# Windowed attention on one core: two PSUM banks for the convolution, attention transposes in the main ring, patch loads among the other transfers, LN transposes one per slot

## The chip, the cores and the metric

The kernel runs on one core of one Trainium2 chip. The metric is the device time of one execution in microseconds (us): the median of two runs before the change is 7355.64 us (7354.11 to 7357.16). All times here are from those runs or from one profiled execution, which took 7363.1 us.

A core has five engines that run their own instruction queues in order: TensorE (PE in the profile; its weight loads are PEld), VectorE (DVE), ScalarE (ACT), GpSimd (POOL) and SyncE (SP), which in this kernel issues the DMA transfers. Engines wait for each other through semaphores. TensorE writes its results to PSUM; VectorE and ScalarE copy them to SBUF.

## The reference

The input is one image of 511 x 511 positions with 192 channels in bf16. A depthwise 3 x 3 convolution is added to it, each position is layer-normalised, and four-headed attention runs inside each of 73 x 73 windows of 7 x 7 positions:

```python
for i in range(kk):                      # kk = 3
    for j in range(kk):
        pe = pe + xp[:, i:i + H, j:j + W, :] * dw_pe[i, j][None, None, None, :]
x0 = x + pe
h = _layernorm(x0, axis=-1)
# ... h cut into windows of 49 positions: hw
qkv = (hw @ w_qkv).reshape(-1, ws * ws, 3, nh, dh)   # 4 heads of 48
attn = jnp.einsum('wnhd,wmhd->whnm', q, k) * scale
attn = _softmax(attn, axis=-1)
out = jnp.einsum('whnm,wmhd->wnhd', attn, v)
out = out.reshape(-1, ws * ws, C) @ w_o
# ... windows put back in place
return x0 + out
```

## The kernel before

Windows are taken in 42 blocks of up to 128, one window per partition. While one block is in attention, the convolution and the normalisation of the next are done beside it, and so is the output projection of the previous one. A block is cut into slots of eight windows, 16 in a full block and 667 in all.

PSUM holds three tiles of two banks in a ring (`PS`), one bank for the attention transposes and one for the convolution:

```python
self.PS = _Rot([psum.tile([128, 1024], F32, name=f"ps{i}") for i in range(3)])
self.PE_ = psum.tile([128, 512], F32, name="pse")
self.PC = psum.tile([128, 512], F32, name="psc")
```

The convolution of one channel is one matmul: the 81 values of a 9 x 9 patch per window against a table `T`. Ten channels fill the bank, and then VectorE copies it out:

```python
def conv_mm(cv):                                            # line 297 is the matmul
    c = cv.c
    mm(PCB[:, (c % 10) * S : (c % 10 + 1) * S], lhsT=XP[0:KP, :, c], rhs=T[0:KP, c, :], start=True, stop=True)
    cv.c += 1
    if cv.c % 10 == 0 or cv.c == C:
        ...
        nc.vector.tensor_copy(                              # line 302
            out=self.X[cv.b % 3][:, :, c0 : c0 + n], in_=PCB[:, 0 : n * S].rearrange("p (c s) -> p s c", s=S))
```

The patches `XP` come by 18 transfers per full block (line 265), all issued together once the convolution of the block in between has been read. The rows of x that are added to the convolution's result come through two buffers `xs` (line 279), and finished rows leave by stores (line 284). All three stand in SyncE's queue in program order.

The normalisation is a list of items, drawn from as the slots go: add a row of x (line 309, VectorE), statistics of two positions (line 313, VectorE), the inverse root by two Newton steps (lines 319 to 328), the multiply (line 336, GpSimd). Then `ln_tr` transposes eight positions on TensorE (line 350), and VectorE and ScalarE each copy one half out (line 359):

```python
def ln_rstd(i0, i1):
    e = nc.gpsimd
    e.tensor_scalar(out=t..., in0=v, scalar1=1.0 / C, scalar2=self.eps, op0=ALU.mult, op1=ALU.add)
    e = nc.vector
    e.tensor_scalar(out=rd.bitcast(I32), ..., op0=ALU.logical_shift_right)
    e.tensor_scalar(out=rd.bitcast(I32), ..., op0=ALU.mult, op1=ALU.add)
    e = nc.gpsimd
    for _ in range(2):
        e.tensor_tensor(out=u, in0=t, in1=rd, op=ALU.mult)
        e.tensor_tensor(out=u, in0=u, in1=rd, op=ALU.mult)
        e.tensor_scalar(out=u, in0=u, scalar1=-0.5, scalar2=1.5, op0=ALU.mult, op1=ALU.add)
        e.tensor_tensor(out=rd, in0=rd, in1=u, op=ALU.mult)
```

The stages of a slot, with what copies each out of PSUM: A (line 371, q then k; ScalarE, line 379), B (line 409, logits; ScalarE's exp into `pt`, line 417), V (line 387; ScalarE, line 395), D (line 430, attention times v; VectorE's reciprocal and multiply into `o`, lines 439 and 440), E (line 453, transposes of `o`; VectorE, line 454), and the projection of four positions (line 465; ScalarE, line 469, then GpSimd's add, line 473). D runs one slot after its B, E two slots after. Between the long matmuls of A, V and projection, `fill` puts convolution matmuls. The order in one slot `g`:

```python
stage_A(b, ck, 0, fill)
stats(0.2)
stage_A(b, ck, 1, fill)
stats(0.4)
stage_E(*groups[g - LE], nc.vector.tensor_copy)             # into the bank pse
for s0 in pj:
    proj(b - 1, s0, fill)
    ... store(b - 1, sdone)                                 # as soon as two rows are projected
stats(0.6)
stage_D()
stats(0.8)
stage_B()
stage_V(b, ck, fill, nc.scalar.copy)
while conv.c < conv_goal:                                   # conv_goal: part(0.0, 0.45, C)
    conv_mm(conv)
stats(1.0)                                                  # s_goal: part(0.47, 0.90, len(n.items))
if f > 0.71:
    n.transpose(7 if f == 1.0 else part(0.60, 1.0, 7))      # all that are due, in a row
if conv.c == C and xp_due:
    load_xp(b + 2)                                          # 18 transfers in a row
    xp_due = False
```

Of the kernel before, what the change touches and what calls it, by code (L numbers as in the profile page):

```python
# [61 lines left out]
class _Kernel:  # L62
    def __init__(self, ctx, tc, x, dw_pe, w_qkv, w_o, out, eps, logit_lim):
# [8 lines left out]
        self.PS = _Rot([psum.tile([128, 1024], F32, name=f"ps{i}") for i in range(3)])  # L72
        self.PE_ = psum.tile([128, 512], F32, name="pse")
        self.PC = psum.tile([128, 512], F32, name="psc")
        for t in self.PS.t + [self.PE_, self.PC]:
            nc.vector.memset(t[:], 0.0)
# [108 lines left out]
    def fast(self, ctx):  # L185
# [32 lines left out]
        mm = nc.tensor.matmul  # L218
        ebf = self.PE_[:].bitcast(BF)

# [9 lines left out]
        def clear(part, p0, n):  # L230

            nc.sync.dma_start(
                out=part[:, p0 : p0 + n, :], in_=bass.AP(tensor=zero.tensor, offset=zero.offset, ap=[list(zero.ap[0]), [0, n], [1, C]])
            )

        def load_xp(b):
            for a0, b0, da, db, n, p0 in blocks[b]:
                left = [0] if b0 == 0 else []
                right = [] if b0 + (n - 1) * db < NWC - 1 else list(range(n)) if da else [n - 1]
                if left and any(ln[1] for bb in blocks[:b] for ln in bb):  # L240
                    clear(XPr[0], p0, n if da else 1)
                if right and b:
                    clear(XPr[8], p0 + right[0], len(right))
                last = a0 + (n - 1) * da
                cuts = [0] + ([1] if da and a0 == 0 else []) + ([n - 1] if da and last == NWR - 1 else []) + [n]
                for i, j in zip(cuts, cuts[1:]):
                    if j <= i:
                        continue
                    top, bot = a0 + i * da == 0, a0 + (j - 1) * da == NWR - 1
                    if top and b:  # L250
                        clear(XP[0:9], p0 + i, j - i)
                    if bot and b:
                        clear(XP[KP - 9 : KP], p0 + i, j - i)
                    pr0, pr1 = (1 if top else 0), (8 if bot else 9)
                    for pc in range(9):
                        q, sh = (WS - 1, -1) if pc == 0 else (0, 1) if pc == 8 else (pc - 1, 0)
                        n0, n1 = i, j
                        if pc == 0 and left:
                            n0 = j if da else i + 1
                        if pc == 8 and right:  # L260
                            n1 = i if da else j - 1
                        if n1 <= n0:
                            continue
                        dims = [[W * C, pr1 - pr0], [WS * C * (W * da + db), n1 - n0], [1, C]]
                        nc.sync.dma_start(  # L265
                            out=XPr[pc, pr0:pr1, p0 + n0 : p0 + n1, :],
                            in_=dram(x, WS * (a0 + n0 * da) - 1 + pr0, WS * (b0 + n0 * db + sh) + q, dims),
                        )

# [25 lines left out]
        def conv_mm(cv):  # L295
            c = cv.c
            mm(PCB[:, (c % 10) * S : (c % 10 + 1) * S], lhsT=XP[0:KP, :, c], rhs=T[0:KP, c, :], start=True, stop=True)  # L297
            cv.c += 1
            if cv.c % 10 == 0 or cv.c == C:
                c0 = c - c % 10  # L300
                n = cv.c - c0
                nc.vector.tensor_copy(  # L302
                    out=self.X[cv.b % 3][:, :, c0 : c0 + n], in_=PCB[:, 0 : n * S].rearrange("p (c s) -> p s c", s=S)
                )
# [10 lines left out]
        def ln_rstd(i0, i1):  # L315
            e = nc.gpsimd
            v = bnst[:, i0:i1, :].rearrange("p a (e f) -> p a e f", f=3)[:, :, :, 2]
            rd, u, t = (z[:, 2 * i0 : 2 * i1] for z in (rstd, tmp1, tmp2))
            e.tensor_scalar(out=t.rearrange("p (a e) -> p a e", e=2), in0=v, scalar1=1.0 / C, scalar2=self.eps, op0=ALU.mult, op1=ALU.add)
            e = nc.vector  # L320
            e.tensor_scalar(out=rd.bitcast(I32), in0=t.bitcast(I32), scalar1=1, scalar2=None, op0=ALU.logical_shift_right)
            e.tensor_scalar(out=rd.bitcast(I32), in0=rd.bitcast(I32), scalar1=-1.0, scalar2=1597463007.0, op0=ALU.mult, op1=ALU.add)
            e = nc.gpsimd
            for _ in range(2):
                e.tensor_tensor(out=u, in0=t, in1=rd, op=ALU.mult)
                e.tensor_tensor(out=u, in0=u, in1=rd, op=ALU.mult)
                e.tensor_scalar(out=u, in0=u, scalar1=-0.5, scalar2=1.5, op0=ALU.mult, op1=ALU.add)
                e.tensor_tensor(out=rd, in0=rd, in1=u, op=ALU.mult)

# [116 lines left out]

        def stage_E(b, ck, eng):
            for kt in range(2):
                for Q in range(2):
# [5 lines left out]
                out=HO[b % 2][0:KT, :, ck * CH : (ck + 1) * CH, 0:S],  # L455
                in_=ebf[0:KT].rearrange("p (k w s) -> p k w s", k=2, s=64)[:, :, :, 0:S],
            )
# [36 lines left out]

        def load_chunk(b, k, tiles):
            tiles[k] = xs.next()
            load_x(b, k, tiles[k])

        groups = [(b, ck) for b in range(NB) for ck in range((count(b) + CH - 1) // CH)]
        NG = len(groups)  # L500
        LD, LE = 1, 2

        class Next:


            def __init__(n_, b):
                n_.b, n_.conv, n_.si, n_.loaded, n_.tr = b, Conv(b), 0, 0, 0
                n_.items, n_.tiles = stat_items(b)
                n_.ready = 0

# [6 lines left out]
            def stats(n_, goal):  # L517
                while n_.si < goal:
                    kind, it = n_.items[n_.si]
                    it()  # L520
                    n_.si += 1
                    if kind == 1:
                        n_.load()
                    n_.ready += kind == 2

            def transpose(n_, goal):
                while n_.tr < min(goal, n_.ready):
                    ln_tr(n_.b, 8 * n_.tr, n_.tr)
                    n_.tr += 1

        load_xp(0)
        n = Next(0)
# [4 lines left out]
        if NB > 1:  # L537
            load_xp(1)
        n.stats(len(n.items))
        n.transpose(7)  # L540

        for g in range(NG + LE + 1):
            b, ck = groups[g] if g < NG else (NB, g - NG)
            f0, f = 0.0, 1.0
            if g < NG:
                nslot = (count(b) + CH - 1) // CH
                f0, f = ck / nslot, (ck + 1) / nslot
            if ck == 0:
                n = Next(b + 1) if b + 1 < NB else None
                xp_due = b + 2 < NB  # L550
                pdone = sdone = 0

            def part(lo, hi, total):
                return min(total, max(0, int((f - lo) / (hi - lo) * total + 0.5)))

            pj = []
            if 1 <= b and ck >= LE:
                goal = 13 if b == NB else part(0.10, 0.70, 13)
                while pdone < goal:
# [3 lines left out]
            conv = n.conv if n else None  # L563
            conv_goal = part(0.0, 0.45, C)
            conv_start = conv.c if n else 0
# [8 lines left out]
            s_start = n.si if n else 0  # L574
            s_goal = part(0.47, 0.90, len(n.items)) if n else 0

            def stats(share):
                if n and conv.c == C:
                    n.stats(int(s_start + (s_goal - s_start) * share))

            if n and f >= 0.3 and n.loaded == 0:
                n.load()
                n.load()

            if g < NG:
                stage_A(b, ck, 0, fill)
                stats(0.2)
                stage_A(b, ck, 1, fill)
                stats(0.4)
            if 0 <= g - LE < NG:  # L590
                stage_E(*groups[g - LE], nc.vector.tensor_copy)
            for s0 in pj:
                proj(b - 1, s0, fill)
                while sdone < len(CHUNKS) and CHUNKS[sdone][1] * WS <= min(S, s0 + 4):
                    store(b - 1, sdone)
                    sdone += 1
                    stored[b - 1] = sdone
            stats(0.6)
            if 0 <= g - LD < NG:
                stage_D()  # L600
            stats(0.8)
            if g < NG:
                stage_B()
                stage_V(b, ck, fill, nc.scalar.copy)
                if n:
                    while conv.c < conv_goal:
                        conv_mm(conv)
                    stats(1.0)
                    if f > 0.71:
                        n.transpose(7 if f == 1.0 else part(0.60, 1.0, 7))  # L610
                    if conv.c == C and xp_due:
                        load_xp(b + 2)
                        xp_due = False

# [242 lines left out]
```

## Time and profile before

| Group | Instructions | Busy us | Mean ns |
|---|---|---|---|
| A, matmuls (line 371) | 5336 | 1825.0 | 478 |
| Convolution, matmuls (line 297) | 8064 | 1557.5 | 238 |
| V, matmuls (line 387) | 5336 | 923.2 | 303 |
| Projection, matmuls (line 465) | 4116 | 784.7 | 328 |
| E, matmuls (line 453) | 5336 | 636.2 | 291 |
| LN transposes, matmuls (line 350) | 4116 | 463.3 | 283 |
| Convolution copy, VectorE (line 302) | 840 | 541.8 | 645 |
| D copy, VectorE (line 440) | 667 | 638.7 | 958 |
| Statistics, VectorE (line 313) | 1050 | 544.8 | 549 |
| LN transpose copy, VectorE (line 359) | 294 | 337.8 | 1149 |
| q copy, ScalarE (line 379) | 667 | 541.7 | 812 |
| LN multiply, GpSimd (line 336) | 294 | 710.7 | 2435 |

Busy time is the sum over one kind of instruction, and the mean is that of one instruction; matmuls overlap each other, so their mean is longer than the step from one to the next. The granted clock of TensorE is a share of its full speed, 0.621 on average over the span. The transfers move 377.07 MB, 51 GB/s on average. A row of the waits names the engine and line that waited, what released it, the total in us, how often, and the longest.

### The profile page before, as it was taken

The numbers are of one execution on the slowest core, as the hardware profiler recorded it, in microseconds if no ns is written. First come the engines' busy times: TensorE is split into PE (matmuls) and PEld (weight loads), VectorE is DVE, ScalarE is ACT, GpSimd is POOL, SyncE is SP. The second block draws the span as 40 slices with busy tenths as digits, with TensorE's granted clock in tenths as the row PEclk, the third lists the DMA queues.
The fourth block names the chain that finished last, engine by engine and source line by source line (L and its number), as shares of the span: only waits on it lengthen the run. The fifth ranks groups of instructions, "written<-read, shape, count | busy, mean of one in ns | idle before, by whom it ended". The sixth has DMA issues, their size and how long they took to land.

```text
span 7363.1 us, 168522 instructions
## 1 busy us (share of the span) xinstructions
PE 5032.6 (68%) x75049; PEld 3971.4 (54%) x75049; DVE 2896.4 (39%) x4859; ACT 2853.6 (39%) x3521; POOL 1939.2 (26%) x2364
## 2 busy tenths in 40 slices
PE   1677777766777777777766777777777666666657
PEld 1555555555555555555555555555555555555445
DVE  4433433434443333334434444333444333333323
ACT  1333434433443433334433434344444333333325
POOL 3122222222222222222222222222222222222214
PEclk9866656665665666665656666555565655656557
DMA  2111212222211111122222211112122211111111
GB/s 61 36 49 49 53 49 53 58 65 60 53 51 49 49 49 49 50 53 53 62 63 60 53 49 49 49 49 53 49 54 62 60 45 46 46 47 47 43 32 39
DMA packets 529715, 377.07 MB, mean 51 GB/s; under 512 B 454181, under 2 KB 454373, under 8 KB 528979
## 3 DMA queue, kind: packets, MB, share of 16 engines
q1 hardware_dynamic: 528531, 365.92, 19.5%
q8 instruction: 589, 9.65, 0.5%
q14 instruction: 147, 1.20, 0.1%
q10 hardware_dynamic: 448, 0.30, 0.0%
HBM read 265.31 MB, written 100.27 MB: 50 GB/s over the span
## 4 chain that ended last, share of the span: by engine, by line
PE 52%; DVE 20%; SPq 16%; POOL 4%; issue 4%; DMA 3%; ACT 2%; DVEq 0%; POOLq 0%; ACTq 0%
PE ps L371 18%; SPq L265 14%; DVE X L302 6%; PE psc L297 6%; PE pse L453 6%; PE ps L387 6%; PE ps L350 6%; PE ps L465 6%; DVE HO L359 5%; DMA xs<-in_x_dram 3%; PE ps L430 3%; DVE HO L454 2%; DVE o L440 2%; POOL X L336 2%; PE ps L409 2%
## 5 line engine op out<-in xcount | busy, mean ns | idle before, releaser
L371 PE MATMUL ps<-HO,Wqk 96*128 96x392 bf16 x5336 | 1825.0, 478 | 992.8 <-DVE o L440 977.7
L297 PE MATMUL psc<-T,XP 81*128 81x49 bf16 x8064 | 1557.5, 238 | 494.4 <-DVE X L302 461.0
L473 POOL TENSOR_TENSOR X<-X,pO 128x768 bf16<-128x768 bf16 (+1 forms) x546 | 863.3, 1588 | 3306.3 <-ACT pO L469 3305.2
L371 PEld LDWEIGHTS <-Wqk 96*128 96x128 bf16 x5336 | 679.4, 132 | 1701.1 <-issue 1501.2
L297 PEld LDWEIGHTS <-XP 81*128 81x128 bf16 x8064 | 1337.0, 178 | 203.8 <-issue 114.1
L379 ACT CAST q<-ps 128x784 bf16<-128x784 f32 x667 | 541.7, 812 | 1403.3 <-PE ps L371 1326.0
L454 DVE COPY HO<-pse 96x784 bf16<-96x784 bf16 x667 | 382.0, 573 | 1559.7 <-PE pse L453 1559.7
L350 PE MATMUL ps<-ident,X 128*96 128x128 bf16 x4116 | 463.3, 283 | 723.1 <-DVE HO L359 423.0
L387 PE MATMUL ps<-Wv,HO 96*128 96x192 bf16 x5336 | 923.2, 303 | 35.3 <-ACT pO L469 35.3
L302 DVE CAST X<-psc 128x490 bf16<-128x490 f32 x840 | 541.8, 645 | 947.6 <-PE psc L297 942.2
L350 PEld LDWEIGHTS <-X 128*96 128x96 bf16 x4116 | 412.6, 175 | 738.2 <-issue 472.3
L465 PE MATMUL ps<-Wo,HO 96*128 96x192 bf16 x4116 | 784.7, 328 | 3.6 <-ACT pO L469 2.9
L395 ACT CAST v<-ps 128x768 bf16<-128x768 f32 x667 | 534.8, 802 | 525.5 <-PE ps L387 431.1
L387 PEld LDWEIGHTS <-HO 96*128 96x128 bf16 x5336 | 588.9, 121 | 252.7 <-issue 217.0
L336 POOL TENSOR_TENSOR X<-X,rstd 128x1536 bf16<-128x1536 bf16 (+1 forms) x294 | 710.7, 2435 | 13.1
L469 ACT CAST pO<-ps 128x768 bf16<-128x768 f32 x504 | 402.4, 799 | 782.8 <-PE ps L465 600.7
L465 PEld LDWEIGHTS <-HO 96*128 96x128 bf16 x4116 | 608.0, 176 | 180.9 <-issue 180.0
L417 ACT ACTIVATE pt<-ps 128x784 bf16<-128x784 f32 x667 | 550.3, 825 | 398.0 <-PE ps L409 396.0
L379 ACT CAST k<-ps 128x784 bf16<-128x784 f32 x667 | 542.2, 813 | 381.1 <-PE ps L371 345.6
L359 ACT COPY HO<-ps 96x1024 bf16<-96x1024 bf16 (+1 forms) x294 | 284.6, 968 | 976.1 <-PE ps L350 976.1
L309 DVE TENSOR_TENSOR X<-X,xs 128x1344 bf16<-128x1344 bf16 x294 | 293.5, 998 | 904.1 <-DMA xs<-in_x_dram 902.5
L440 DVE TENSOR_TENSOR o<-ps,rs 128x768 bf16<-128x768 f32 x667 | 638.7, 958 | 23.4
(59 smaller groups left out, 4163.1 us busy)
## 6 DMA issues: line engine op xcount, KB each, us to landing
XP<-in_x_dram SPq DMA_DIRECT2D x568, 216.0 KB
xs<-in_x_dram SPq DMA_DIRECT2D x574, 168.0 KB
out_dram<-X SPq DMA_DIRECT2D x246, 336.0 KB
XP<-in_x_dram SPq DMA_DIRECT2D x151, 212.6 KB
out_dram<-X SPq DMA_DIRECT2D x82, 168.0 KB
XP<-in_x_dram SPq DMA_DIRECT2D x16, 192.0 KB
XP<-in_x_dram SPq DMA_DIRECT2D x64, 30.4 KB
xs<-in_x_dram SPq DMA_DIRECT2D x63, 23.6 KB
```

What stands on the lines that cost most here:

```text
L265: nc.sync.dma_start(out=XPr[pc, pr0:pr1, p0 + n0 : p0 + n1, :], in_=dram(x, WS * (a0 + n0 * da) - 1 + pr0, WS * (b0 + n0 * db + sh) + q, d ...
L297: mm(PCB[:, (c % 10) * S : (c % 10 + 1) * S], lhsT=XP[0:KP, :, c], rhs=T[0:KP, c, :], start=True, stop=True)
L302: nc.vector.tensor_copy(out=self.X[cv.b % 3][:, :, c0 : c0 + n], in_=PCB[:, 0 : n * S].rearrange("p (c s) -> p s c", s=S))
L336: nc.gpsimd.tensor_tensor(out=hbuf(b)[:, s0:s1, :], in0=self.X[b % 3][:, s0:s1, :], in1=rstd[:, i : i + n].unsqueeze(2).to_broadcast([128, ...
L350: mm(pb[0:KT, kt * 1024 + i * 128 : kt * 1024 + (i + 1) * 128], lhsT=h[:, s0 + i, kt * KT : (kt + 1) * KT], rhs=ident[:], start=True, stop ...
L359: eng(out=HO[b % 2][0:KT, kt, :, s0 : s0 + N], in_=pb[0:KT, kt * 1024 : kt * 1024 + N * 128].rearrange("p (s w) -> p w s", w=128),)
L371: mm(ps[:, ab * 512 : ab * 512 + TOK], lhsT=self.Wqk[kt][0:KT, which * 2 + ab, :], rhs=HO[b % 2][0:KT, kt, ck * CH : (ck + 1) * CH, 0:S], ...
L379: nc.scalar.copy(out=dst[:, :, 0:TOK], in_=two_bank(ps, TOK))
L387: mm(ps[:, col : col + C], lhsT=HO[b % 2][0:KT, kt, w : w + 2, :].rearrange("p w s -> p (w s)"), rhs=self.Wv[kt][0:KT, :], start=(kt == 0) ...
L440: nc.vector.tensor_tensor(out=o_[:].rearrange("p b q (h d) -> p b (q h) d", d=DH), in0=ov[:, :, :, 0:DH], in1=r_[:].rearrange("p (b g) -> ...
L465: mm(ps[:, col : col + C], lhsT=HO[b % 2][0:KT, kt, :, s0 + i], rhs=self.Wo[kt][0:KT, :], start=(kt == 0), stop=(kt == 1))
L473: nc.gpsimd.tensor_tensor(out=xv, in0=xv, in1=o[:, 0:n, :], op=ALU.add)
```

## The change

The bank of the attention transposes is given to the convolution, which then alternates between two banks, and E takes a tile of the main ring. The patch loads become a generator whose transfers are issued a few at a time, from 0.44 to 0.92 of a block, and stores go out at the end of the slot that projected their rows. LN transposes go one per slot, before B, and only at least 0.9 slot after their multiply. The inverse root moves from GpSimd to VectorE, three fused instructions to a Newton step where there were four. The shares of the block for convolution, statistics and projection change a little. The purpose is that TensorE is not kept from its next matmuls by a copy, a burst or a queue.

The diff, cut to its core:

```diff
-        self.PE_ = psum.tile([128, 512], F32, name="pse")
-        self.PC = psum.tile([128, 512], F32, name="psc")
+        self.PC = _Rot([psum.tile([128, 512], F32, name=f"psc{i}") for i in range(2)])
...
         def load_xp(b):                                     # now a generator, clear() too
-                        nc.sync.dma_start(out=XPr[...], in_=dram(x, ...))
+                        yield lambda dst=dst, src=src: nc.sync.dma_start(out=dst, in_=src)
...
         def conv_mm(cv):
             c = cv.c
+            if c % 10 == 0:
+                cv.ps = PCB.next()
-            mm(PCB[:, (c % 10) * S : (c % 10 + 1) * S], lhsT=XP[0:KP, :, c], rhs=T[0:KP, c, :], ...)
+            mm(cv.ps[:, (c % 10) * S : (c % 10 + 1) * S], lhsT=XP[0:KP, :, c], rhs=T[0:KP, c, :], ...)
...
         def ln_rstd(i0, i1):
-            e = nc.gpsimd
+            e = nc.vector
             e.tensor_scalar(out=t..., in0=v, scalar1=1.0 / C, scalar2=self.eps, ...)
...
-            e = nc.gpsimd
             for _ in range(2):
-                e.tensor_tensor(out=u, in0=t, in1=rd, op=ALU.mult)
+                e.scalar_tensor_tensor(out=u, in0=rd, scalar=-0.5, in1=t, op0=ALU.mult, op1=ALU.mult)
                 e.tensor_tensor(out=u, in0=u, in1=rd, op=ALU.mult)
-                e.tensor_scalar(out=u, in0=u, scalar1=-0.5, scalar2=1.5, op0=ALU.mult, op1=ALU.add)
-                e.tensor_tensor(out=rd, in0=rd, in1=u, op=ALU.mult)
+                e.scalar_tensor_tensor(out=rd, in0=u, scalar=1.5, in1=rd, op0=ALU.add, op1=ALU.mult)
...
         def stage_E(b, ck, eng):
+            ebf = PS.next()[:].bitcast(BF)
...
-            def transpose(n_, goal):
-                while n_.tr < min(goal, n_.ready):
+            def transpose(n_, goal, age):
+                if n_.tr < min(goal, len(n_.ready)) and n_.ready[n_.tr] + age <= now[0]:
                     ln_tr(n_.b, 8 * n_.tr, n_.tr)
...
-            s_goal = part(0.47, 0.90, len(n.items)) if n else 0
+            s_goal = part(0.46, 0.82, len(n.items)) if n else 0
-            def stats(share):
+            def hook(share):
+                nonlocal xpn, sdone
+                at = f0 + (f - f0) * share
                 if n and conv.c == C:
                     n.stats(int(s_start + (s_goal - s_start) * share))
+                    if n.loaded < min(WS, n.added + 2):
+                        n.load()
+                while sq and sq[0][0] <= g + share:
+                    _, bb, k = sq.pop(0)
+                    store(bb, k)
+                    stored[bb] = k + 1
+                if conv is None or conv.c == C:
+                    goal = part(0.44, 0.92, len(xp), at)
+                    while xpn < goal:
+                        xp[xpn]()
+                        xpn += 1
...
+            late = f0 >= 0.44
             if g < NG:
                 stage_A(b, ck, 0, fill)
-                stats(0.2)
+                hook(0.15)
+            if 0 <= g - LE < NG:
+                stage_E(*groups[g - LE], nc.scalar.copy if late else nc.vector.tensor_copy)
+            if g < NG:
                 stage_A(b, ck, 1, fill)
-                stats(0.4)
-            if 0 <= g - LE < NG:
-                stage_E(*groups[g - LE], nc.vector.tensor_copy)
+                hook(0.35)
+            if 0 <= g - LD < NG:
+                stage_D()
             for s0 in pj:
                 proj(b - 1, s0, fill)
-                    store(b - 1, sdone)
+                    sq.append((g + 0.9, b - 1, sdone))
-            stats(0.6)
-            if 0 <= g - LD < NG:
-                stage_D()
-            stats(0.8)
+            hook(0.55)
             if g < NG:
+                if n:
+                    n.transpose(part(0.56, 0.96, 7), 0.9)
                 stage_B()
+                hook(0.75)
                 stage_V(b, ck, fill, nc.scalar.copy)
...
-                    if f > 0.71:
-                        n.transpose(7 if f == 1.0 else part(0.60, 1.0, 7))
-                    if conv.c == C and xp_due:
-                        load_xp(b + 2)
-                        xp_due = False
+                    if f == 1.0:
+                        while n.tr < 7:
+                            n.transpose(7, -9.0)
```

## The prediction

> **What bounds the kernel now.** I read four views: the page's totals and clock row, the waits of TensorE and VectorE, the timeline of the queues in one steady block, and windows of that block. [...]Counting from one copy of q to the same copy 16 slots later, blocks 2 to 39 take 173.4 us on average. The page's totals first:
>
> ```profile
> PE 5032.6 (68%) x75049; PEld 3971.4 (54%) x75049; DVE 2896.4 (39%) x4859; ACT 2853.6 (39%) x3521; POOL 1939.2 (26%) x2364
> PEclk9866656665665666665656666555565655656557
> DMA  2111212222211111122222211112122211111111
> ```
>
> No engine is full, and TensorE's clock is near half. So I ask which waits stop TensorE, and what the engines that it names were waiting for:
>
> ```profile
> PE ps L371 <- DVE o L440: 977.7, 123, 64.9
> PE psc L297 <- DVE X L302: 461.0, 716, 1.2
> PE ps L350 <- DVE HO L359: 423.0, 294, 22.7
> PE ps L350 <- POOL X L336: 254.8, 42, 37.3
> ...
> DVE X L309 <- DMA xs<-in_x_dram: 902.5, 41, 67.1
> DVE rstd L321 <- POOL tmp L319: 147.7, 85, 7.9
> ```
>
> The first row is not arithmetic on VectorE: VectorE runs in order and stands for a row of x (fifth row, 41 times, 22 us each: once per block). Why is that row late? The SyncE queue and VectorE of one block say it:
>
> ```profile
> 3162.90 24.92 SPq L265 DMA_DIRECT2D XP<-in_x_dram  x18
> 3187.93 3.15 SPq L279 DMA_DIRECT2D xs<-in_x_dram  x4
> ...
> 3194.45 0.86 DVE L309 TENSOR_TENSOR X<-X,xs 128x1344 bf16<-128x1344 bf16 x1 [19.63 <-DMA xs<-in_x_dram]
> 3198.04 2.44 PE L371 MATMUL ps<-HO,Wqk 96*128 96x392 bf16 x7 [17.36 <-DVE o L440]
> ```
>
> Eighteen patch loads take the queue for 24.92 us, the row goes out behind them, the add starts, and TensorE resumes after 17.36 us. Then the block's two other regimes, LN (first row) and convolution (second):
>
> ```profile
> 3198.00:3252.00 54.00, 36.51 (x553) 27.13 (x553) 25.77 (x44) 22.74 (x28) 17.09 (x32) 0.71 0.10 27
> 3082.00:3157.00 75.00, 64.02 (x872) 52.33 (x872) 24.45 (x40) 29.36 (x37) 11.50 (x7) 0.50 0.09 20
> ```
>
> The columns are window, length, busy PE, PEld, DVE, ACT, POOL, clock, DMA share, GB/s. In the convolution TensorE is 85% busy, and all of it at half clock. In LN it waits a third of the time.
>
> **What the Trainium skill says.** "TensorE: Matmul & The Clock Gate", Part 1, has the clock at 4/8 or 8/8, decided by activity in windows of about 3.4 us. The trace agrees: its clock records are only 0.5 (5583 us in all) and 1.0 (1502 us), with changes on a grid of 3.41 us. The section there on psum-queue cycling says that micro-idling between bursts keeps the clock oscillating; the 0.50 beside the 461.0 us of bank waits fits. "Perfetto Trace Analysis", Matmuls, advises rotating independent groups through PSUM banks so that the evacuation of one lies beside the next; the single psc bank breaks that, and line 297 waits after nearly every group of ten. "DMA: Bandwidth & Descriptors", Issuing engines are not separate DMA queues, calls the issuing time usually small beside the transfer. Here the trace differs: issuing is the 24.92 us that delays the row.
>
> I counted, for each 3.41 us interval of this trace at half clock, the moving columns of its matmuls except the convolution's (small 49-column ones of B and D at a quarter, as four share the array). Half clock moves 1.19 columns per ns (392+49 in 0.37 us), some 4070 in an interval. Taking 4096 as 1, full clock followed in none of the 1210 intervals below 0.8, in 20% of 143 from 0.8 to 0.9, in 53% of 150 from 0.90 to 0.95 and in 126 of 127 above. With the convolution's columns counted in, 160 intervals of convolution reach 0.80 to 0.95 and none was followed by full clock; of 179 such intervals without convolution, 76 were. So the clock wakes only when the queue is nearly solid, and convolution columns seem not to count.
>
> **The change, part by part.** Each wait is per kernel, in us.
>
> 1. Second psc bank. A copy of ten channels is 645 ns, and the next ten matmuls spread over some 3.3 us between long ones. Even if VectorE does D's evacuation first (252 + 958 ns), the bank is free again in time. Removes 440 of 461.
>
> 2. Patch loads in pieces from 0.44 to 0.92 of the block, stores put off, and each row loaded when its buffer is released. The number of issues stays, but never more than two or three stand ahead of a row. Of the 977.7, about 800 go; slots 8 and 9 have 4.75 us per block of this wait with VectorE busy, and 42 blocks of that, 200, stay. Left over: 178, so I take off 800.
>
> 3. LN transposes one per slot, at least 0.9 slot after their normalisation, in place of bursts of up to four. A burst waits 1.3 us at each for the 1149 ns copy, and once 5.4 us for the multiply on GpSimd. Of 423 + 255 I leave 100: minus 580.
>
> 4. E in the main ring, after the first A. It frees the bank for part 1. The ring of three tiles now has eight users per slot, not seven; every tile still has two other groups of matmuls before reuse, and the copies are 0.6 to 1.2 us. But D, not E and D, now stands between k's matmuls and B. With no projection and no LN transpose in the slot (two to four of 16), B waits for k's 813 ns copy behind 0.45 us of D: about 0.5 us each, 42 blocks x 3 x 0.5 = plus 60. In the second half of a block E's copy goes to ScalarE (estimate 0.8 us, from its 812 ns for 784 columns), 336 times: 270 busy, beside TensorE.
>
> 5. Inverse root on VectorE. GpSimd loses 321 us busy; VectorE gains 7 instructions x 168 x about 0.18 (its two neighbours take 166 and 174 ns) = 210, and loses its 147.7 wait. This lies where VectorE is fullest. Per slot of the LN stretch (5.8 slots): 7 adds x 1.00 + 25 statistics x 0.55 + 36 small x 0.18 = 27 us, so 4.7, plus D 1.2 and the transposed half 1.15: 7.05. The stretch becomes VectorE's; I add 3 us per block, plus 125.
>
> Sum: 7356 - 440 - 800 - 580 + 60 + 125 = 5721. Denser intervals should wake the clock a little more: 10% of about 75 us of convolution per block at full clock would save some 3 us per block, minus 125. **I predict 5600 us.**
>
> As a check, a block moves 16 x 5696 columns for A, V and E, 12,544 for LN transposes, 18,816 for projection and 9408 for convolution: 131,904, at 1.19 per ns 111 us, plus 16 us for B and D. All at half clock with no gap: 127 us, or 41.7 x 127 + 240 (start and tail) = 5530. So 5600 is nearly solid half clock, or some gaps paid for with full clock. The steady block would be 131 us.
>
> **Rivals.** (a) *The clock wakes in the convolution.* A, E, A in a row without bank waits is 3.84 us at half clock, 90% of it counted columns, just longer than an interval. Against: all columns at the very threshold, and D and B lower it in every slot. If half of that stretch ran at full clock: 5100 to 5250. (b) *VectorE takes over as the bound of LN,* and slots there take 9 to 9.5 instead of 8 us: 42 x 8 x 1.3 = 440 more, about 6050. For it: 7.05 of 8 us in an in-order engine. (c) *The SyncE queue still stands still,* because a store waits for GpSimd's add (this queue shows 4037 us of such waits) with rows and patches behind it. Half of the 800 would stay, or convolution would wait for its last patch: 6000 to 6200. Against: in the new order a store goes out at the end of the slot, after its add of 1.6 us. (d) *The gaps were hidden anyway,* with the clock dropping as they fill: under 2%. Against: the waits named stop TensorE itself, and the clock is already at 0.5 there.
>
> **Range and chances.** (a) sets the low end, (b) and (c) the high one: 5200 to 6150. Even with both (b) and (c) it stays 1000 us below the present time, so faster by over 2% has 0.96; 0.02 each for the others, for a stop that I do not see.
>
> **What would show it.** Right: line 297 waits under 50 us; VectorE's wait for xs under 150; the LN transposes' waits under 150; slot 10 near 8 us, not 27; convolution slots 1 to 2 us shorter. The granted clock between 0.60 and 0.70. GpSimd near 1620 us busy, ScalarE near 3120, VectorE near 2900. Wrong: a new wait of TensorE on XP or on a ring tile of over 300 us, or a clock above 0.75.

## The result and the profile after

The changed kernel takes 5470.35 us, the median of two runs (5465.18 to 5475.52). The ratio to the kernel before is 0.7437, with a 95% interval of 0.7405 to 0.7469. The prediction was 5600 us with a range of 5200 to 6150. The total was close by luck, because two errors cancelled: the convolution stretch gained far more than predicted, and the LN stretch far less.

The totals of the changed kernel and its clock row, from its page:

```profile
PE 4474.0 (82%) x75049; PEld 3649.1 (67%) x75049; DVE 3264.3 (60%) x5701; ACT 3060.1 (56%) x3855; POOL 1649.9 (30%) x852
...
PEclk9977777777777777777777777777777777777777
DMA  2222222232333322222222333322222232233211
```

TensorE runs the same 75049 matmuls in less busy time, because the granted clock went from 0.621 to 0.765 on average. Its waits and VectorE's, then (rows as before: who waited for whom, total us, times, longest):

```profile
PE ps L347 <- DVE HO L356: 665.8, 294, 24.2
...
PE ps L384 <- DVE o L437: 112.8, 45, 2.8
...
DVE X L309 <- DMA xs<-in_x_dram: 41.7, 7, 23.4
...
PE ps L347 <- POOL X L333: 35.5, 1, 35.5
...
PE ps L368 <- DVE o L437: 2.4, 2, 1.5
```

Of the four waits of TensorE shown before, three are gone or small. A (line 368 now) stands 2.4 us behind D's copy, where it stood 977.7, and V (line 384) has 112.8 of that wait. The convolution no longer waits for its bank at all (461.0 us before; there is no such row now). VectorE's wait for a row of x fell from 902.5 to 41.7 us, and the LN transposes' wait for GpSimd's multiply from 254.8 to 35.5. The fourth grew: the LN transposes (line 347 now) wait 665.8 us for VectorE's copy, 423.0 before. SyncE's queue around the same place of a block shows how the rows got ahead of the patches:

```profile
2509.32 1.67 SPq L266 DMA_DIRECT2D XP<-in_x_dram  x2
2511.09 1.41 SPq L277 DMA_DIRECT2D xs<-in_x_dram  x2
2512.55 1.66 SPq L266 DMA_DIRECT2D XP<-in_x_dram  x2
2514.30 2.82 SPq L277 DMA_DIRECT2D xs<-in_x_dram  x2
2517.17 1.66 SPq L266 DMA_DIRECT2D XP<-in_x_dram  x2
```

Here no more than two patch loads stand ahead of a row. The block's last nine go out in one run, after the last row and store (12.15 us from 2533.75 in this block). The two regimes of the block, as windows of the changed kernel (LN first, then convolution; window, length, busy PE, PEld, DVE, ACT, POOL, clock, DMA share, GB/s):

```profile
2534.80:2591.80 57.00, 43.38 (x645) 32.56 (x644) 28.12 (x50) 28.72 (x36) 9.34 (x5) 0.65 0.16 41
2598.00:2634.00 36.00, 35.87 (x736) 32.96 (x734) 20.89 (x34) 25.56 (x35) 14.73 (x9) 1.00 0.23 61
```

The first window runs on into the first slots of the next block, and the second begins in slot 2. From there the convolution runs at 1.00, with hardly any idle TensorE, where it ran at 0.50 before. Over slots 0 to 6 of the steady blocks, full clock has 78% of the time, and had 4% before. That is the largest part of the gain. LN sits at 0.65 with a quarter of the time idle.

The table sums the slots of a steady block, blocks 2 to 39, in us, from one ScalarE copy of q to the next, for this kernel and the experiments below. Slots 0 to 6 hold the convolution, 7 to 9 the passage, 10 to 15 most of LN.

| Kernel | Time, us | Slots 0-6 | 7-9 | 10-15 | Block |
|---|---|---|---|---|---|
| before | 7355.64 | 71.7 | 22.2 | 79.4 | 173.4 |
| after | 5470.35 | 45.3 | 21.7 | 59.6 | 126.6 |
| one convolution bank | 6497.85 | 72.9 | 19.9 | 58.5 | 151.3 |
| two banks only | 6168.50 | 43.4 | 23.3 | 77.6 | 144.4 |
| patches at once | 6356.41 | 47.6 | 20.9 | 80.1 | 148.7 |
| root on GpSimd | 5472.89 | 47.7 | 18.6 | 60.5 | 126.8 |
| LN transposes in bursts | 5648.54 | 47.0 | 19.0 | 64.8 | 130.8 |
| multiply in pieces | 5583.56 | 49.6 | 20.5 | 59.6 | 129.7 |
| both halves first | 5057.22 | 46.8 | 19.5 | 50.8 | 117.1 |
| and ScalarE's copy first | 5046.18 | 47.1 | 19.9 | 49.4 | 116.3 |
| and both copies on ScalarE | 5064.72 | 50.2 | 20.7 | 47.0 | 117.9 |
| and E's copy on VectorE | 5087.74 | 48.9 | 20.0 | 49.5 | 118.3 |
| E second, three roots | 4831.17 | 44.8 | 21.5 | 44.2 | 110.6 |

### The profile page after: what moved, and what is told of

Same layout as the page of the kernel before. It is cut to its first block, busy times and chain, and to the rows that moved or that the text cites. A ratio compares the mean times of both kernels' runs of the same rounds, so it can differ in the third digit from the quotient of the medians.

```text
span 5473.7 us, 168639 instructions
## 1 busy us (share of the span) xinstructions
PE 4474.0 (82%) x75049; PEld 3649.1 (67%) x75049; DVE 3264.3 (60%) x5701; ACT 3060.1 (56%) x3855; POOL 1649.9 (30%) x852
## 4 chain that ended last, share of the span: by engine, by line
PE 69%; DVE 18%; issue 5%; ACT 3%; SPq 2%; POOL 1%; DMA 1%; DVEq 0%; POOLq 0%; ACTq 0%
PE ps L368 22%; PE ps L384 12%; PE ps L463 9%; PE ps L451 8%; PE psc L297 6%; DVE HO L356 5%; PE ps L406 5%; PE ps L347 4%; PE ps L427 4%; DVE o L437 3%; DVE bnst L313 3%; DVE X L309 3%; SPq L266 2%; DVE rs L436 2%; ACT k L376 1%
## 5 line engine op out<-in xcount | busy, mean ns | idle before, releaser
L368 PE MATMUL ps<-HO,Wqk 96*128 96x392 bf16 x5336 | 1652.7, 429 | 19.0 <-ACT HO L356 15.4
L297 PEld LDWEIGHTS <-XP 81*128 81x128 bf16 x8064 | 1241.7, 186 | 148.1 <-issue 44.8
L297 PE MATMUL psc<-T,XP 81*128 81x49 bf16 x8064 | 1288.6, 209 | 38.1 <-DMA xs<-in_x_dram 31.8
L347 PE MATMUL ps<-ident,X 128*96 128x128 bf16 x4116 | 424.1, 259 | 710.9 <-DVE HO L356 665.8
L384 PE MATMUL ps<-Wv,HO 96*128 96x192 bf16 x5336 | 872.0, 302 | 118.6 <-DVE o L437 112.8
L368 PEld LDWEIGHTS <-Wqk 96*128 96x128 bf16 x5336 | 629.0, 125 | 297.2 <-issue 244.1
L347 PEld LDWEIGHTS <-X 128*96 128x96 bf16 x4116 | 347.3, 151 | 717.2 <-issue 670.3
L436 DVE RECIPROCAL rs<-ps 128x16 f32<-128x16 f32 x667 | 169.2, 254 | 962.9 <-PE ps L427 909.8
L384 PEld LDWEIGHTS <-HO 96*128 96x128 bf16 x5336 | 615.1, 123 | 161.0 <-issue 112.3
L463 PE MATMUL ps<-Wo,HO 96*128 96x192 bf16 x4116 | 703.6, 307 | 12.8 <-ACT HO L452 9.3
L463 PEld LDWEIGHTS <-HO 96*128 96x128 bf16 x4116 | 633.4, 180 | 23.1 <-issue 3.5
L451 PEld LDWEIGHTS <-o 128*96 128x96 bf16 x5336 | 532.2, 167 | 108.2 <-issue 52.6
```

Source lines behind the costliest of these rows:

```text
L297: mm(cv.ps[:, (c % 10) * S : (c % 10 + 1) * S], lhsT=XP[0:KP, :, c], rhs=T[0:KP, c, :], start=True, stop=True)
L347: mm(pb[0:KT, kt * 1024 + i * 128 : kt * 1024 + (i + 1) * 128], lhsT=h[:, s0 + i, kt * KT : (kt + 1) * KT], rhs=ident[:], start=True, stop ...
L368: mm(ps[:, ab * 512 : ab * 512 + TOK], lhsT=self.Wqk[kt][0:KT, which * 2 + ab, :], rhs=HO[b % 2][0:KT, kt, ck * CH : (ck + 1) * CH, 0:S], ...
L384: mm(ps[:, col : col + C], lhsT=HO[b % 2][0:KT, kt, w : w + 2, :].rearrange("p w s -> p (w s)"), rhs=self.Wv[kt][0:KT, :], start=(kt == 0) ...
L451: mm(ev, lhsT=o_[:, sl, Q, kt * KT : (kt + 1) * KT], rhs=ident[:], start=True, stop=True, is_transpose=True)
L463: mm(ps[:, col : col + C], lhsT=HO[b % 2][0:KT, kt, :, s0 + i], rhs=self.Wo[kt][0:KT, :], start=(kt == 0), stop=(kt == 1))
```

## The experiments

The theory after the result: (1) the second bank removes waits that kept TensorE's activity under the level at which the clock wakes; (2) the pieces end the wait for x; (3) the LN slots are set by the wait of an LN tile's second half for VectorE's copy of the first, and by the half clock that goes with it. Each expectation gives the rival beside it.

### One convolution bank, the rest of the change kept

```diff
-        self.PC = _Rot([psum.tile([128, 512], F32, name=f"psc{i}") for i in range(2)])
+        self.PC = _Rot([psum.tile([128, 512], F32, name=f"psc{i}") for i in range(1)])
```

> The changed kernel, with one convolution bank in place of two and all else kept. If the single bank's waits are what keeps TensorE's clock at half speed in the convolution stretch, slots 0 to 6 go from 45 us back to 65 to 70 us at half clock, the mean clock to about 0.65 and the time to 6300 to 6600 us. If the new order of stages (A, E, A in a row) is what woke the clock and the bank costs its wait alone, the stretch stays at full clock and the time grows by at most the 461 us that the bank cost before: under 5930 us.

6497.85 us; the ratio to the kernel before is 0.882 (0.8806 to 0.8835). Its waits of TensorE and a window of its convolution stretch:

```profile
PE psc L297 <- DVE X L302: 391.1, 670, 0.9
```

```profile
2899.90:2972.60 72.70, 63.05 (x866) 50.62 (x865) 25.11 (x40) 28.61 (x36) 13.18 (x8) 0.55 0.11 30
```

The first expectation holds, with slots 0 to 6 a little above the 65 to 70 us given. The waits add to 391 us, yet the kernel is 1027 us slower than with two banks, and all of that is in slots 0 to 6 (72.9 for 45.3 us; the others are 3 us shorter). Full clock has 8% of the time there, against 78% with two banks. So the bank's waits cost over twice their own length, through the clock. The new order of stages alone hardly wakes it.

### Two banks only, on the kernel before

```diff
-        self.PE_ = psum.tile([128, 512], F32, name="pse")
-        self.PC = psum.tile([128, 512], F32, name="psc")
+        self.PC = _Rot([psum.tile([128, 512], F32, name=f"psc{i}") for i in range(2)])
...                                    # conv_mm takes the next bank every ten channels
         def stage_E(b, ck, eng):
+            ebf = PS.next()[:].bitcast(BF)
```

> The kernel before, with two convolution banks and E in the main ring at its old place, and nothing else. If the banks tip the clock, slots 0 to 6 go from 71.7 to 45 to 50 us, the mean clock to 0.70 or more and the time to 6200 to 6350 us; slot 10 keeps its 27 us. If the banks only take their wait away, the convolution stays at half clock and the time is about 6900 us.

6168.5 us; ratio 0.8372 (0.8346 to 0.8398). This part of the change alone brings 1187 us of its 1885. Slots 0 to 6 take 43.4 us, a little less than with the whole change. The window is one convolution stretch of this kernel:

```profile
2742.00:2772.00 30.00, 28.89 (x619) 27.99 (x617) 17.07 (x28) 20.43 (x26) 11.49 (x7) 0.97 0.10 26
```

The window runs from slot 2 into slot 7 of one block. In the old order of stages too, the stretch is solid and at full clock for 76% of slots 0 to 6. The time is a little under the first expectation, whose theory holds. The two experiments together show the cause: the bank, and not the rest, decides it.

### Patch loads at once

```diff
-                    goal = part(0.44, 0.92, len(xp), at)
+                    goal = len(xp)
```

> The changed kernel, but all patch loads of a block are issued at the first opportunity after the convolution, in one go. If issuing in pieces is what ended the wait for the row of x, VectorE waits some 15 to 20 us per block for it again and the time is 6000 to 6250 us. If asking for rows two ahead already hides the 25 us of issuing, the time is within 100 us of 5470.

6356.41 us; ratio 0.8644 (0.8614 to 0.8674), 886 us slower than the changed kernel, more than the range that I gave. The queue and VectorE in one of its blocks:

```profile
2830.18 24.56 SPq L266 DMA_DIRECT2D XP<-in_x_dram  x18
2854.84 8.85 SPq L277 DMA_DIRECT2D xs<-in_x_dram  x6
```

```profile
2861.69 0.86 DVE L309 TENSOR_TENSOR X<-X,xs 128x1344 bf16<-128x1344 bf16 x1 [20.46 <-DMA xs<-in_x_dram]
```

The wait of before is back, 957.4 us over the kernel against 902.5, and slot 10 is 31.1 us instead of 10.0. Asking for rows two ahead does not hide 24.56 us of issuing.

### Inverse root back on GpSimd

```diff
         def ln_rstd(i0, i1):
-            e = nc.vector                       # nine instructions
+            e = nc.gpsimd                       # two of eleven on VectorE, as before the change
```

> The changed kernel, with the inverse root split over GpSimd and VectorE as before. If VectorE bounds the LN stretch, its busy time falls from 3264 us to about 2950 and the time by 2 to 4%, to 5250 to 5360 us. If the handing over between the two engines costs more than the work, VectorE waits for GpSimd again and LN transposes come late: 5550 to 5700 us.

5472.89 us; ratio 0.7428 (0.7416 to 0.7441): the same time as the changed kernel. Neither expectation held. VectorE's busy time fell by 488 us, from 3264.3 to 2776.8, and the LN slots did not get shorter (60.5 for 59.6). But a wait in the midst of the root came back:

```profile
DVE rstd L321 <- POOL tmp L319: 329.4, 127, 7.8
```

Less work and more waiting can have cancelled, so this run alone does not show that VectorE's load leaves the LN slots unchanged. It shows that where the root runs makes no difference to the time.

### LN transposes in bursts

```diff
-                    n.transpose(part(0.56, 0.96, 7), 0.9)      # before B, one per slot
...
+                    if f > 0.71:                               # behind V, all that are due
+                        while n.transpose(7 if f == 1.0 else part(0.60, 1.0, 7), -9.0):
+                            pass
```

> The changed kernel, with the LN transposes in bursts behind V in the last 30% of the block and with no minimum age, as before the change. If one per slot is what saved the waits of before (423 us for VectorE's copy, 255 for GpSimd's multiply), about 300 us come back: 5700 to 5850 us. If a transpose in a slot pays the same wait for its own copy wherever it stands, the time stays within 150 us of 5470; with the multiply's wait less than 100 us as the statistics end earlier than before.

5648.54 us; ratio 0.7667 (0.7651 to 0.7683). One per slot, with its place before B and its minimum age, is worth 178 us, or 3.3% of 5470, between what the two theories gave. The wait of the transposes for VectorE's copy is 792.6 us here and 665.8 one per slot: both come 294 times, once per tile.

### Both halves of an LN transpose before their copies

In each tile, eight matmuls transpose the first half of the channels, VectorE copies them out, then come eight for the second half and ScalarE's copy. In the timeline the second eight start only once VectorE is done, although they fill the tile's other bank. One slot of the changed kernel, TensorE, then VectorE:

```profile
2546.28 0.65 PE L347 MATMUL ps<-ident,X 128*96 128x128 bf16 x8
2550.67 1.01 PE L347 MATMUL ps<-ident,X 128*96 128x128 bf16 x8 [3.74 <-DVE HO L356]
2551.61 0.63 PE L406 MATMUL ps<-q,k 48*64 48x49 bf16 x32
```

```profile
2546.48 0.26 DVE L436 RECIPROCAL rs<-ps 128x16 f32<-128x16 f32 x1 [3.63 <-PE ps L427]
2546.77 0.96 DVE L437 TENSOR_TENSOR o<-ps,rs 128x768 bf16<-128x768 f32 x1
...
2549.40 1.21 DVE L356 COPY HO<-ps 96x1024 bf16<-96x1024 bf16 x1
```

TensorE stands 3.74 us in the midst of one tile, behind D's copy, nine small root instructions and the copy itself. The edit:

```diff
             for kt in range(2):
                 for i in range(N):
                     mm(pb[0:KT, ...], lhsT=h[...], rhs=ident[:], ..., is_transpose=True)
+            for kt in range(2):
                 eng = nc.vector.tensor_copy if kt == 0 else nc.scalar.copy
```

> The changed kernel, with the 16 LN transposes of a tile issued before its two copies, where the second eight waited for VectorE's copy of the first. If that wait (2.3 us per tile, 666 us in all) with the half clock it brings sets the LN slots, TensorE's wait goes under 100 us, slots 10 to 15 go from 59.6 us to 45 to 50 us, more of them at full clock, and the time is 4850 to 5150 us. If VectorE's own work or its wait for GpSimd's port sets them, the wait only moves to the next tile and the time stays above 5350 us.

5057.22 us; ratio 0.6854 (0.6829 to 0.6878). This is 413 us, or 7.6%, under the changed kernel, for one added line, and the first expectation holds. Slots 10 to 15 go from 59.6 to 50.8 us, just short of the 45 to 50 given, and the clock over the kernel is 0.841. What is left, from its waits, first ScalarE's and then TensorE's:

```profile
ACT HO L357 <- DVE HO L357: 826.5, 250, 110.8
...
PE ps L369 <- ACT HO L357: 351.7, 242, 3.4
```

The two copies of a tile still follow each other, so ScalarE, and the next A that needs the tile, wait for VectorE.

### GpSimd's multiply in pieces

VectorE's add of a row takes 840 ns where no GpSimd instruction runs and about 2.32 us on average where one does (some 160 of the 287 adds after the first block, changed kernel). In one block of it, GpSimd and VectorE:

```profile
2549.63 5.46 POOL L333 TENSOR_TENSOR X<-X,rstd 128x1536 bf16<-128x1536 bf16 x2 [11.46 <-DVE rstd L325]
```

```profile
2551.11 1.28 DVE L319 TENSOR_SCALAR tmp<-bnst 128x2 f32<-128x2 f32 x1
2552.43 2.67 DVE L320 TENSOR_SCALAR rstd<-tmp 128x2 int32<-128x2 int32 x1
2555.14 0.17 DVE L321 TENSOR_SCALAR rstd<-rstd 128x2 int32<-128x2 int32 x1
```

Two elements per partition take 2.67 us, and the instruction ends at 2555.10 us, as the second of the two multiplies does (2549.63 + 5.46 = 2555.09). The Trainium skill, "SBUF — State Buffer", Who interferes with whom, says that VectorE and GpSimd share a port pair, and that of two instructions which both need it the first to issue holds it to its end. The times above agree, and the edit tries the length of the multiply:

```diff
-            nc.gpsimd.tensor_tensor(out=hbuf(b)[:, s0:s1, :], ...)                     # eight positions
+            for d in range(0, n, 4):
+                nc.gpsimd.tensor_tensor(out=hbuf(b)[:, s0 + d : s0 + d + m, :], ...)   # m = 4
```

> The changed kernel, with GpSimd's LN multiply in pieces of four positions, not eight: the same work in twice as many instructions of some 1.25 us. If VectorE's long adds (2.3 us where a GpSimd multiply runs, 0.84 us elsewhere) wait for the multiply's end, the long ones fall to about 1.6 us and VectorE's busy time by 150 to 200 us. If it is bandwidth that the two share, their means stay. Since VectorE does not set the slots (root on GpSimd took 490 us from it and left the time), the time stays within 100 us of 5470.

5583.56 us; ratio 0.7571 (0.7553 to 0.7589). The adds beside GpSimd fell to 1.65 us and the long small root instruction from 2674 ns to 1391, which is what waiting for the end of one instruction gives; bandwidth shared by the element would not change with the pieces. But the next instruction of that root (173 ns in the changed kernel) now takes 1390 ns too, beside the next piece, so that root got no shorter, and VectorE's busy time fell by 94 us, less than I gave. The time rose by 113 us, outside the 100 given, and not in LN (59.6 us in both): slots 0 to 6 take 49.6 for 45.3. The changed kernel is at full clock from slot 1 on in all 38 steady blocks; here that comes in slot 1, 2 or 4 (7, 15 and 16 blocks). Why it does is open.

### Both halves, and the root on GpSimd

```diff
+            for kt in range(2):                 # both halves first, as above
...
+            e = nc.gpsimd                       # the root as before the change
```

> The changed kernel, with both halves of an LN transpose before their copies and the inverse root back on GpSimd. If VectorE becomes the bound of the LN stretch once the wait of the halves is gone, this is 100 to 300 us faster than the halves alone. If something else sets the slots then, such as ScalarE's copies or TensorE itself, it is within 60 us of them.

Four executions took 5184 us once and 5271 to 5279 us three times, the latter in a slower state that recurs, so only the first is compared: 127 us slower than both halves alone, by this one execution. Neither expectation held. The root stays on VectorE.

### The order and the engines of the two copies

First, ScalarE copies the first half and VectorE the second:

```diff
-                eng = nc.vector.tensor_copy if kt == 0 else nc.scalar.copy
+                eng = nc.scalar.copy if kt == 0 else nc.vector.tensor_copy
```

> Both halves of an LN transpose before their copies, as in the run before, with the first copy on ScalarE and the second on VectorE (the two copies of one tile follow each other, and ScalarE waited 827 us for VectorE's). If ScalarE held up by VectorE, and with it exp and the next A, is what is left in the LN slots, slots 10 to 15 go from 50.8 us to about 43 and the time to 4700 to 4850 us. If the tile's release by the slower of the two copies is what counts, whichever comes first, the time stays within 60 us of 5057.

5046.18 us; ratio 0.6842 (0.6818 to 0.6866): not different from both halves alone (0.6829 to 0.6878), and the second expectation holds in its time. ScalarE no longer waits for VectorE there. The stop moved to V, which needs D's tile back:

```profile
PE ps L385 <- DVE o L438: 359.2, 131, 4.2
PE ps L369 <- DVE HO L357: 187.4, 187, 2.1
```

Then both copies on ScalarE:

```diff
-                eng = nc.scalar.copy if kt == 0 else nc.vector.tensor_copy
+                eng = nc.scalar.copy
```

> The same, with both copies of an LN transpose on ScalarE. VectorE loses 335 us of busy time and nothing on ScalarE waits for it, but ScalarE has some 6 to 7 us per LN slot. If VectorE's delays set the LN slots, 4650 to 4800 us; if ScalarE becomes the bound, 4900 us or more.

5064.72 us; ratio 0.6864 (0.6835 to 0.6893). The time is in the second range, but not for its reason: slots 10 to 15 are shorter, 47.0 us, and slots 0 to 6 are 50.2, as the clock wakes late again and eats the gain. Last, E's copy on VectorE as well:

```diff
-                stage_E(*groups[g - LE], nc.scalar.copy if late else nc.vector.tensor_copy)
+                stage_E(*groups[g - LE], nc.vector.tensor_copy)
```

> The same, with E's copy on VectorE in the whole block. ScalarE loses 333 copies of 0.86 us (286 us) and VectorE takes 190. If ScalarE bounds the LN slots in the run before this, 50 to 150 us faster than it; if VectorE's delays come back through E's copy, 50 to 200 us slower.

5087.74 us; ratio 0.6902 (0.6877 to 0.6926), which overlaps the run before it, so neither expectation held. All four versions with both halves first lie within 1%: moving the copies between engines mostly changed who waits.

### E behind the second A in the convolution, and three roots

In the run with ScalarE's copy first, slot 13 held a wait of V of 3.1 us per block for D's copy. Before it on VectorE stands the last small root, held by GpSimd:

```profile
2345.12 1.29 DVE L319 TENSOR_SCALAR tmp<-bnst 128x2 f32<-128x2 f32 x1
2346.44 2.67 DVE L320 TENSOR_SCALAR rstd<-tmp 128x2 int32<-128x2 int32 x1
...
2350.70 0.96 DVE L438 TENSOR_TENSOR o<-ps,rs 128x768 bf16<-128x768 f32 x1
```

```profile
2351.72 1.44 PE L385 MATMUL ps<-Wv,HO 96*128 96x192 bf16 x8 [3.15 <-DVE o L438]
```

Two edits, each in other slots: that root is joined to the third, and E goes behind the second A where the convolution runs.

```diff
-                    if i % 8 == 7 or i == 24:
+                    if i in (7, 15, 24):
+                        k0 = min(i // 8, 2) * 8          # the last group takes statistics 16 to 24
...
-            if 0 <= g - LE < NG:
+            if late and 0 <= g - LE < NG:
                 stage_E(...)
             if g < NG:
                 stage_A(b, ck, 1, fill)
                 hook(0.35)
+            if not late and 0 <= g - LE < NG:
+                stage_E(*groups[g - LE], nc.vector.tensor_copy)
```

> The run with ScalarE's copy first, and two edits that show in different slots. In the convolution stretch E stands behind the second A, as before the change, so that B has more than D between itself and k's copy; and the inverse root comes in three groups, the last one with what were the third and fourth. If the waits of B for k (0.3 us in slots 0 and 1) with their half clock cost what the slots show, slots 0 and 1 go from 6.7 and 6.6 us to about 6.1 and the stretch wakes sooner: slots 0 to 6 from 47.1 us to 43 to 45. If the last small root, held up by GpSimd's multiply, is what stops V in slot 13, its 3.1 us there go and slots 10 to 15 go from 49.4 to about 46. Both: 4750 to 4900 us. If the wake only wanders and the wait finds another holder, within 60 us of 5046.

4831.17 us; ratio 0.6569 (0.6545 to 0.6593). This is the fastest kernel of the study, 11.7% under the changed one, and it lands where expected. Slot 13 went from 8.8 to 6.0 us with no such wait, and no root instruction runs beside a multiply any more; slots 10 to 15 lost 5.2 us per block. Slots 0 and 1 take 12.75 us together for 13.30, and slots 2 and 3 are at full clock for 92% of their time, not 58%; slots 0 to 6 lost 2.3 us. As the two edits ran together, their shares are read from the slots alone. The share of E's place is not shown even so: the changed kernel, with E before the second A, takes 45.3 us for slots 0 to 6, as little as this one within 0.5 us, so the wake may only have wandered.

## Why the prediction was right, and where it was not

**Second bank.** Right in its wait (440 of 461 predicted, all 461 gone) and wrong by far in its size. Slots 0 to 6 lost 26.4 us per block, of which the bank's waits in the kernel before are 10.9. The other 15.5 us x 41.7 blocks are some 650 us, where the sum has 125 for the clock.

The step that failed is "10% of about 75 us of convolution per block at full clock". It lets the stretch wake for a moment now and then. What the runs show is one wake per block that then holds itself. In the changed kernel it comes in slot 1 of all 38 steady blocks and lasts until slot 8, where TensorE stands 2.8 us for D's copy. Nor did the clock oscillate in this stretch before, as the prediction reads the Trainium skill's section on psum-queue cycling: it stayed at half for 96% of the time. Full clock moves more columns in the same time: its intervals of 3.41 us with at least six convolution matmuls hold 1.32 times 4096 columns on average, 1.14 even without the convolution's own, and 402 of 404 were followed by full clock again. Rival (a), given the low end of the range, is what happened.

The step under it, "convolution columns seem not to count", is too strong, but they do not count in full either. Counted as in the prediction, with each matmul's columns shared out over the time of its record: in the changed kernel at half clock, none of 81 intervals with at least six convolution matmuls and under 0.90 in all was followed by full clock, and 40 of the 42 at 0.90 and above were. Those that woke hold 0.81 to 0.84 without the convolution, where none of 46 intervals free of it woke in the two kernels. Yet in the thirteen kernels of the table, 495 intervals at half clock reach 0.90 only with these columns and hold under 0.80 without, and one of them was followed by full clock. So how much they count stays open.

**Patches in pieces.** Minus 800 predicted; putting them back at once costs 886. Right, by the mechanism given.

**LN transposes.** Minus 580 predicted; the two waits named are 701 us after and 678 before. The step "A burst waits 1.3 us at each for the 1149 ns copy" took the wait for one of the burst. It is one of the tile, between its own halves, and a slot of its own pays it too; issuing both halves first took 413 us off. The wait grew to 2.26 us per tile (665.8 / 294, for 423.0 / 294 = 1.44); in the slot shown above, D's copy and nine root instructions stand ahead of the copy. The multiply's wait did go. One per slot is worth 178 us by experiment.

**Main ring for E.** Plus 60 for B's wait; that row is 21 us in the changed kernel. Whether it has a price through the clock in slots 0 and 1 is not shown: the last experiment changed two things, and its gain there may be the wandering of the wake.

**Root on VectorE.** Busy 210 more was predicted. VectorE rose by 368 in all, though half of E's copies left it (191 us): adds are 197 us longer (490.9 for 293.5), and two of the nine small ones take 799 and 455 ns on average where I took 180, because GpSimd's multiply holds some of them. The 125 us that I put on the time for it are zero on balance: back on GpSimd, the time is the same.

**LN stretch.** "slots there take 9 to 9.5 instead of 8 us" was rival (b), and they take 9.9 (59.6 / 6). Its reason, a full VectorE, fits at most some slots: VectorE is busy for 9.4 of 10.0 us in slot 10, but slots 13 and 14 have 2.9 and 2.4 us of its work and take 8.9 and 9.0. They are the wait of about 2 us plus matmuls at mostly half clock, some 35% of the time at full. What set the stretch is the wait inside the tile, with the clock that it cost: without it the six slots take 50.8 us.

So the range held by cancelling, which is luck. The convolution stretch gave some 1100 us (26.4 x 41.7) where the sum has 565 (440 and 125), and all the rest some 785 of the 1885 where it has 1190. By its own test, "a clock above 0.75" (0.765 came), the prediction's account of the clock was wrong. Three signs of being right are missing too: the LN transposes' waits are not under 150 us but 701, slot 10 takes 10.0 us, not near 8, and VectorE is busy for 3264 us, not 2900.

Left open: which slot the convolution stretch wakes in. It took 43.4 to 50.2 us in kernels with two banks that do the same work there. The clock's grid of 3.41 us and the density of slots 0 and 1 may both play into it, and no run separates them.

## What to carry to other kernels

A wait of half a microsecond that recurs every few microseconds on TensorE can cost more than its length if it keeps the clock from waking: here 391 us of waits cost 1027. So look at the granted clock by stage, and count on a jump, not on the sum of the waits. Where a transpose tile has two halves and two copies, try to issue all its matmuls first. And count the transfers that stand ahead of the one you need in its queue, as issuing eighteen took 25 us.

## What the runs showed of the hardware

- In intervals of 3.41 us without convolution, kernels before and after together, full clock followed half clock after none of 704 with under 0.85 of 4096 moving columns and after all 272 with 0.95 or more. It was kept after 1 of 463 and all 134 of such intervals at full clock. So the level lies at about the same count at either speed in these traces, as a correlation. It is not exact: in the run with E's copy on VectorE, 13 of 28 intervals at 0.75 to 0.80 kept full clock. "TensorE: Matmul & The Clock Gate", Part 1, tells of the windows and the two states.
- A VectorE instruction on two elements per partition took 2.67 us, not 0.17, while GpSimd multiplied; with the multiply halved in length it took 1.39. Statistics (549 ns without GpSimd, 548 beside its multiply), the reciprocal of D's sums (254 and 257) and D's multiply from PSUM (957 in both) were not held.
